# Attention beside a gated MLP on one core: early down products, P.V held for zero products, and two output tiles summed by DMA

## The chip, the cores and the metric

The kernel runs on one core of a Trainium2 chip. The metric is the device time of one execution in microseconds. The engines have their own instruction queues: TensorE (PE, with its weight loads shown as PEld), VectorE (DVE), ScalarE (ACT), GpSimd (POOL) and SyncE (SP). Each takes its instructions in the order in which the program was built; between engines, and between an engine and a DMA, semaphores hold an instruction until what it needs is there.

## The reference

```python
# x: (1, 2048, 640) bf16; wqkv 640x1920, wo 640x640; w_gate, w_up 640x1728, w_down 1728x640
xn = layernorm(x)
# A: 32 heads of 20 columns, full softmax over 2048 keys
q, k, v = split(xn @ wqkv)
s = (softmax(q @ k.T * 20**-0.5) @ v) @ wo
# B: gated MLP
h = sigmoid(xn @ w_gate) * (xn @ w_up)
g = silu(h @ w_down)
out = x + s * g
```

## The kernel before

The 2048 tokens are four chunks of 512 queries, the 32 heads eight groups of four. A **pass** is one chunk with one group: 64 **banks** of scores, each 128 keys of one head by the chunk's 512 queries, in one bank of PSUM. TensorE computes the scores (`score`, L1280), in rounds of three banks and of two in turn (the tiles `sc`). ScalarE takes the exp of a round in one instruction (L1306). Some banks go one at a time to a shared bank (`spare`), and VectorE evaluates the exp by a polynomial in four instructions (L1326, L1347, L1351, L1357). The product of the probabilities with V (P.V, `pv`, L1483) adds all 16 key tiles of a pass into one bank, `oacc`; column 0 of V is one, so that its row holds the denominator. Then VectorE copies `oacc` (L804), the denominators go through DRAM to be inverted and spread (L808 to L824), and L836 scales.

Everything else is a **job**, a generator that gives TensorE's work in small steps: k, q and v projections; `gateup_job` (the gate and the up product of 128 of the 1728 columns of the MLP for one chunk: L667; tanh on ScalarE L679; VectorE's product into `hT`, L688); `down_job` (a 512-column slice of h @ w_down, one bank with 14 products for each piece, L717; tanh L726, VectorE L729, a store to DRAM L731); `out_job` (output projection of an earlier chunk, L751, multiplied by the stored gate value L757, and added by DMA into an output that already holds x, L759). Jobs share two banks of PSUM (`misc0` and `misc1`, `take_bank`) with the `spare` banks of VectorE's exps. The last of a chunk pair's 14 gate and up tiles, 64 columns wide, is computed for two chunks at once, so odd chunks have it from the even chunk before.

The order of all this is not written out: a planner at build time (the loop from L1514) keeps modelled clocks of TensorE, ScalarE and VectorE, and prices in ns (L365 on, `mm_time` L695). At each turn it issues the next round of scores if ScalarE will run dry, else a step of a job (`fill`), a bank for VectorE, a batch of eight P.V products (`pv_batch`), or a product of zeros (`zero_add`, L1454). Zero products keep TensorE's clock up: they are added when less than 2500 ns of products streamed in the last 3400 ns (`streamed`). They go into `oacc` while it has an open sum of P.V (L1459); if all P.V of the pass is issued and `oacc` is not yet copied, they go into an unused shared bank (L1465). `spare_wanted` (L468) keeps one of the two shared banks back from jobs when a round is near, for VectorE.

The last chunk is special, so that little stays behind the last exp. Its gate values stay in SBUF (`gq_last`), in space of `kT_all`. `part_job` multiplies the output projection of the first five groups by the gate for each of four tiles of 128 tokens into `ahead` (two halves of 320 columns, L783 and L788) and adds x by a GpSimd DMA (L791). The last pass is split into parts of 256, 128 and 128 queries (`PARTS`); `last_job` normalises a part on chip (copy of `oacc` L895 or, for the last, L897 on ScalarE; transposes of it L922, inverse L928, spreading L933, product L950, scaling L957), then multiplies the last three groups' projection (`out_mm`, L912) by the gate in halves (`gated`, L997) or, for the last tile, in one (L979). `summed` (L1001) adds `ahead` on VectorE, casts to bf16, and SyncE stores the tile (L1002).

Of the kernel before, what the change touches and what calls it, by code (L numbers as in the profile page):

```python
# [12 lines left out]
ALU = mybir.AluOpType  # L13
# [45 lines left out]
def kernel(  # L59
# [304 lines left out]

    MM5, MM3, MM1 = 216.0, 136.0, 70.0  # L365
    INTO = {"score": 100.0, "pv": 100.0, "fill": 100.0}
    WINDOW, ENOUGH, ZEROS, RESTED = 3400.0, 2500.0, 16, 400.0
    PE_OUT, SEM = 260.0, 70.0
    EXP_COL, EXP_FIX, EXP_LAG = 1 / 1.2, 52.0, 260.0
    DMA_WAIT, LANDED = 3400.0, 4000.0  # L370
# [97 lines left out]
    def spare_wanted():  # L468

        free = sum(c.t is not None and c.t <= pe[0] for c in banks)  # L470
        return (free == 1 and not pressed() and next_round[0] - pe[0] < (KEEP_SPARE if at_bank[0] < SPARE_END else KEEP_LATE)
                and dve.backlog + dve.t - next_round[0] < D_BACKLOG)

    EARLY = 2
# [218 lines left out]
            h_cells.setdefault(c + k, []).append(tnh_free[-1])  # L693

    def mm_time(n):  # L695
        return max(n / 2.4 + 3.0, 100.0)

    def down_pieces(k):
        return [(t4, max(t4 * D, k * QC), min((t4 + 1) * D, (k + 1) * QC)) for t4 in range(QC // P)
# [2 lines left out]
    def down_job(c, k):  # L702
        last = c == NQC - 1
        yield "known", lambda: (bulk[0] == NFT and pe[0] > bulk_t[0] + LANDED and len(h_cells.get(c, [])) == NFT
                                and (not last or front() >= PER_PASS * (NG * c + k // 2 + 1)))
        yield "wait", h_cells[c]
        hT = hTs[c]
        if last:
            gq = gq_last[:, k * QC:(k + 1) * QC]
        else:  # L710
            gq = glu[0].tile([P, QC], FP32, tag="gqr", bufs=4, name="gq")
        held, psd = yield "bank",
        for t4, f0, f1 in down_pieces(k):
            for kf in range(NFT):
                rows = slice(0, P) if kf < NFT - 1 else slice(EDGE * (c % 2), EDGE * (c % 2 + 1))
                h_in = hT[:, kf, :] if kf < NFT - 1 else hEs[c]
                nc.tensor.matmul(psd[:, f0 - k * QC:f1 - k * QC], lhsT=h_in[rows, t4 * P:(t4 + 1) * P],  # L717
                                 rhs=glu[1][rows, kf, f0 - t4 * D:f1 - t4 * D], start=(kf == 0), stop=(kf == NFT - 1),
                                 skip_group_check=True)
                yield "mm", mm_time(f1 - f0), (f1 - f0) / 2.4  # L720
        d_cells.setdefault(c, []).append(Cell(pe[0]))
        made = {}

        def tanh():
            made["t"] = wk.tile([P, QC], BF16, tag="tnh", bufs=2, name="td")
            nc.scalar.activation(out=made["t"], in_=psd, func=ACT.Tanh, scale=0.25)  # L726

        def finish():
            nc.vector.scalar_tensor_tensor(out=gq, in0=made["t"], scalar=1.0, in1=psd, op0=ALU.add, op1=ALU.mult)  # L729
            if not last:  # L730
                nc.gpsimd.dma_start(out=gq_dram[c, :, k * QC:(k + 1) * QC], in_=gq)  # L731

        turned = act.add(480.0, [Cell(pe[0] + PE_OUT + 100.0), *tnh_free[-2:-1]], tanh, 0, EXP_LAG)
        tnh_free.append(dve.add(606.0, [turned], finish, 1))
        give_bank(held, tnh_free[-1])
        gq_cells[c, k] = tnh_free[-1]
# [168 lines left out]
    def last_job(u):  # L905
        q0, width = PARTS[u]
        part, n, final = taken_parts[u], width // P, u == len(PARTS) - 1
        tiles = range(q0 // P, (q0 + width) // P)
        qc, made = NQC - 1, {}

        def out_mm(ps, t4, h, g):
            nc.tensor.matmul(ps, lhsT=oTs[qc, g][:, t4 * P:(t4 + 1) * P], rhs=wo_pad[:, g, h * HALF:(h + 1) * HALF],  # L912
                             start=(g == PRE), stop=(g == NG - 1), skip_group_check=True)

        yield "wait", [part["cell"]]
        if final:
            side = psum.tile([P, 3, 512], FP32, tag="sc0", bufs=1, name="side")
            pd, prl = side[:, 0, :], side[:, 1, :]
        else:
            held, pd = yield "bank",  # L920
        for k in range(n):
            nc.tensor.matmul(pd[:, k * P:(k + 1) * P], lhsT=part["oev"][:, k * P:(k + 1) * P], rhs=identf,  # L922
                             start=True, stop=True, skip_group_check=True)
            yield "mm", 330.0, 200.0

        def invert():
            made["rq"] = wk.tile([P, n, GH], FP32, tag="den", bufs=2, name="rq")
            nc.vector.reciprocal(out=made["rq"].rearrange("p t j -> p (t j)"), in_=pd[:, 0:n * P:P // GH])  # L928

        def spread():  # L930
            made["rb"] = glu[0].tile([P, QC], FP32, tag="gqr", bufs=4, name="rb")[:, 0:n * P].rearrange(
                "p (t j i) -> p t j i", t=n, j=GH)
            nc.vector.tensor_copy(out=made["rb"], in_=made["rq"].unsqueeze(3).to_broadcast([P, n, GH, 32]))  # L933

        cell = dve.add(160.0, [Cell(pe[0] + PE_OUT)], invert, -1)
        if not final:
            give_bank(held, cell)
        cell = dve.add(70.0 + n * P, [cell], spread, -1)
        if final:
            spread_last.append(cell)  # L940
            outs = psum.tile([P, 2, 512], FP32, tag="sc1", bufs=1, name="outs")
            for h in range(2):
                for g in range(PRE, NG - 1):
                    out_mm(outs[:, h, 0:HALF], tiles[0], h, g)
                    yield "mm", MM3
        yield "wait", [cell]
        if not final:
            held, prl = yield "bank",
        for k in range(n):
            nc.tensor.matmul(prl[:, k * P:(k + 1) * P], lhsT=made["rb"][:, k, :, :].rearrange("p j i -> p (j i)"),  # L950
                             rhs=identf, start=True, stop=True, skip_group_check=True)
            yield "mm", 330.0, 200.0

        def scale():
            if steps[-1] not in oTs:
                oTs[steps[-1]] = wk.tile([P, QC], BF16, tag="oT", bufs=NG + 3, name="oT")
            nc.vector.tensor_tensor(out=oTs[steps[-1]][:, q0:q0 + width], in0=part["oev"], in1=prl[:, 0:width],  # L957
                                    op=ALU.mult)

        cell = dve.add(70.0 + width, [Cell(pe[0] + PE_OUT)], scale, -1)  # L960
        if not final:
            give_bank(held, cell)
        yield "known", lambda: all((NQC - 1) * 4 + t4 in out_cells for t4 in tiles)
        yield "wait", [cell, ot_cells[steps[-2]]]
        for k, t4 in enumerate(tiles):
            got = []
            if final:
                if k:
                    outs = psum.tile([P, 3, 512], FP32, tag="sc0", bufs=1, name="outs")
                    for h in range(2):  # L970
                        out_mm(outs[:, h, 0:HALF], t4, h, NG - 2)
                        yield "mm", MM3
                for h in range(2):
                    out_mm(outs[:, h, 0:HALF], t4, h, NG - 1)
                    yield "mm", MM3

                def gate(t4=t4, outs=outs):
                    gq = gq_last[:, t4 * D:(t4 + 1) * D].rearrange("p (h d) -> p h d", h=2)
                    nc.vector.scalar_tensor_tensor(out=gq, in0=outs[:, 0:2, 0:HALF], scalar=0.25, in1=gq,  # L979
                                                   op0=ALU.mult, op1=ALU.mult)  # L980

                got.append(dve.add(740.0, [Cell(pe[0] + PE_OUT)], gate, -1))
            else:
                for h in range(2):
                    held, ps = yield "bank",
                    for g in range(PRE, NG):
                        out_mm(ps[:, 0:HALF], t4, h, g)
                        yield "mm", MM3
                    got.append(dve.add(400.0, [Cell(pe[0] + PE_OUT)], lambda t4=t4, h=h, ps=ps: gated(t4, h, ps), 1))
                    give_bank(held, got[-1])  # L990
                got.append(ending)
            dve.add(740.0, [out_cells[(NQC - 1) * 4 + t4], *got],
                    lambda t4=t4: summed(t4), -1 if final else 2)

    def gated(t4, h, ps):
        gq = gq_last[:, t4 * D:(t4 + 1) * D][:, h * HALF:(h + 1) * HALF]
        nc.vector.scalar_tensor_tensor(out=gq, in0=ps[:, 0:HALF], scalar=0.25, in1=gq, op0=ALU.mult, op1=ALU.mult)  # L997

    def summed(t4):
        ot = glu[0].tile([P, QC], FP32, tag="gqr", bufs=4, name="ot").bitcast(BF16)[:, 0:D]  # L1000
# [513 lines left out]
    while pv_pass[0] < len(steps) - 1 + len(PARTS):  # L1514
# [37 lines left out]
        if b0 < NB and not stuck and alone(room):  # L1552
            idle = False
            credit = min(credit + per_bank(b0), 3000.0)
            continue
        batch = pv_batch()
        cost = PV_TIME + (INTO["pv"] if mode[0] != "pv" else 0.0)
        if batch and (cost <= room or held >= HELD):
            pv(batch)
# [62 lines left out]
```

## Time and profile before

| what | value |
|---|---|
| median of 3 runs | 879.56 us (878.5 to 880.36) |
| profiled execution | 878.75 us, its span 877.1 us |
| busy: TensorE, VectorE, ScalarE, GpSimd | 799.4, 837.9, 861.9, 170.0 us |
| exps on ScalarE (L1306) | 711: 355 of three banks, 356 of two |
| exps on VectorE (L1326) | 271 instructions |
| zero products, built | 163 into `oacc` (L1459), 6 into a shared bank (L1465) |
| mean granted TensorE clock | 0.999 |

The span is the time from the first to the last instruction of the profiled execution. Times in the profile's views are microseconds from the span's start. A line of a timeline gives start, length, engine, source line, operation, the tiles written and read, and in brackets the idle time before it with what ended it. Instructions of one engine overlap a little, so a step from start to start is shorter than a length.

### The profile page before, as it was taken

The numbers are of one execution on the slowest core, as the hardware profiler recorded it, in microseconds if no ns is written. First come the engines' busy times: TensorE is split into PE (matmuls) and PEld (weight loads), VectorE is DVE, ScalarE is ACT, GpSimd is POOL, SyncE is SP. The second block draws the span as 40 slices with busy tenths as digits, with TensorE's granted clock in tenths as the row PEclk, the third lists the DMA queues.
The fourth block names the chain that finished last, engine by engine and source line by source line (L and its number), as shares of the span: only waits on it lengthen the run. The fifth ranks groups of instructions, "written<-read, shape, count | busy, mean of one in ns | idle before, by whom it ended". The sixth has DMA issues, their size and how long they took to land.

```text
span 877.1 us, 16778 instructions
## 1 busy us (share of the span) xinstructions
PE 799.4 (91%) x6358; PEld 286.2 (33%) x6440; DVE 837.9 (96%) x1164; ACT 861.9 (98%) x832; POOL 170.0 (19%) x314
## 2 busy tenths in 40 slices
PE   8999899999998999999999999989989989999997
PEld 3434333332222333222223332232223332233344
DVE  7799999999999999999999999999999999999996
ACT  7999999999999999999999999999999999999996
POOL 8401111101111113211101133111112231111110
PEclk9999999999999999999999999999999999999999
DMA  8212231125542124223321235313211443320111
GB/s 320 62 49 66 72 108 36 33 59 142 155 130 68 28 68 108 38 59 74 73 60 39 68 83 86 72 29 84 57 35 50 101 71 80 71 52 21 26 34 47
DMA packets 107303, 63.86 MB, mean 73 GB/s; under 512 B 78674, under 2 KB 101030, under 8 KB 107130
## 3 DMA queue, kind: packets, MB, share of 16 engines
q1 hardware_dynamic: 95270, 46.96, 20.1%
q0 software_dynamic: 11952, 15.83, 8.5%
q8 instruction: 50, 0.82, 0.4%
q14 instruction: 31, 0.25, 0.1%
HBM read 49.94 MB, written 16.11 MB: 75 GB/s over the span
## 4 chain that ended last, share of the span: by engine, by line
ACT 64%; issue 17%; PE 11%; DVE 6%; DMA 1%; POOL 0%; SPq 0%; ACTq 0%; DVEq 0%; POOLq 0%
ACT p L1306 60%; PE sc L1280 3%; ACT tnh L679 3%; PE work L667 2%; PE work L717 2%; PE oacc L1483 2%; DVE du L1351 1%; DVE dy L1326 1%; ACT td L726 1%; DVE p L1357 1%; DVE du L1347 1%; DMA x_sb<-in_A_x_dram 1%; DVE stats L261 1%; POOL x_sb L284 0%; PE oacc L1459 0%
## 5 line engine op out<-in xcount | busy, mean ns | idle before, releaser
L1306 ACT ACTIVATE p<-sc 128x1536 bf16<-128x1536 f32 x711 | 823.1, 1382 | 1.3 <-PE sc L1280 1.2
L1280 PE MATMUL sc<-qT,kT_all 21*128 21x512 bf16 (+2 forms) x1892 | 278.1, 369 | 55.1 <-ACT p L1306 48.0
L1326 DVE TENSOR_SCALAR dy<-spare 128x512 f32<-128x512 f32 x271 | 184.9, 683 | 14.2 <-PE spare L1280 12.0
L1280 PEld LDWEIGHTS <-kT_all 21*128 21x128 bf16 x2176 | 90.4, 91 | 293.8 <-issue 282.5
L1351 DVE SCALAR_TENSOR_TENSOR du<-du,dy 128x1024 f32<-128x1024 f32 (+1 forms) x166 | 169.3, 1021 | 1.3
L1347 DVE SCALAR_TENSOR_TENSOR du<-dy 128x1024 f32<-128x1024 uint16 (+1 forms) x159 | 168.5, 1060 | 1.2
L1357 DVE SCALAR_TENSOR_TENSOR p<-du,dy 128x1024 uint16<-128x1024 f32 (+1 forms) x152 | 167.2, 1100 | 1.4
L1483 PE MATMUL oacc<-p,v_all 128*21 128x512 bf16 (+2 forms) x2176 | 157.2, 370 | 0.6 <-issue 0.3
L1280 PE MATMUL spare<-qT,kT_all 21*128 21x512 bf16 (+2 forms) x284 | 103.7, 373 | 0.5 <-issue 0.3
L808 POOL DMA_DIRECT2D den_dram<-oev x30 | 18.0, 600 | 354.1 <-DVE oev L804 342.7
L717 PE MATMUL work<-wd,hT 128*128 128x512 bf16 (+3 forms) x410 | 75.2, 301 | 1.9 <-DVE dy L1326 1.2
L667 PE MATMUL work<-xnT,wg 128*128 128x512 bf16 (+1 forms) x262 | 74.0, 383 | 1.9 <-issue 0.6
L667 PE MATMUL work<-xnT,wu 128*128 128x512 bf16 (+1 forms) x266 | 69.8, 381 | 2.1 <-DVE dy L1326 0.6
L824 POOL DMA_DIRECT2D rl<-rec_dram x120 | 60.9, 544 | 52.2 <-DMA rec_dram<-den 47.4
L1483 PEld LDWEIGHTS <-v_all 128*21 128x21 bf16 x2176 | 31.8, 90 | 59.3 <-issue 57.3
L1459 PE MATMUL oacc<-xnT,zero 128*128 128x512 bf16 x124 | 42.7, 385 | 3.0 <-issue 2.4
L717 PEld LDWEIGHTS <-hT 128*128 128x128 bf16 x416 | 30.7, 97 | 39.0 <-issue 29.7
L818 POOL DMA_DIRECT2D rec_dram<-den x30 | 16.4, 547 | 132.9 <-DVE den L817 125.1
L679 ACT ACTIVATE tnh<-work 128x512 bf16<-128x512 f32 x54 | 39.3, 728 | 0.0
L138 PE MATMUL work<-xnT,wqd 128*120 128x512 bf16 (+1 forms) x115 | 35.0, 393 | 0.6 <-DVE hT L688 0.3
L688 DVE SCALAR_TENSOR_TENSOR hT<-tnh,work 128x512 bf16<-128x512 bf16 x52 | 35.3, 679 | 0.1
L667 PEld LDWEIGHTS <-wu 128*128 128x128 bf16 (+1 forms) x280 | 23.4, 98 | 36.7 <-issue 18.8
(132 smaller groups left out, 573.7 us busy)
## 6 DMA issues: line engine op xcount, KB each, us to landing
wg<-in_B_w_gate_dram SPq DMA_DIRECT2D x52, 160.0 KB
wu<-in_B_w_up_dram SPq DMA_DIRECT2D x52, 160.0 KB
rl<-rec_dram POOLq DMA_DIRECT2D x120, 64.0 KB, 2.5
qT<-q_dram SPq DMA_DIRECT2D x31, 128.0 KB
gq_dram<-gq POOLq DMA_DIRECT2D x15, 256.0 KB, 2.3
gqr<-gq_dram SPq DMA_DIRECT2D x15, 256.0 KB
kT_all<-k_dram SPq DMA_DIRECT2D x28, 128.0 KB
wd<-in_B_w_down_dram SPq DMA_DIRECT2D x13, 160.0 KB
```

Of the source, the lines that this page charges most:

```text
L667: nc.tensor.matmul(ps[EDGE * k:EDGE * (k + 1), :] if both else ps, lhsT=w[:, kd, 0:EDGE if both else P], rhs=xnT[:, kd, (c + k) * QC:(c + ...
L679: nc.scalar.activation(out=made["t"][0:fsz, :], in_=psg[0:fsz, :], func=ACT.Tanh, scale=0.5)
L717: nc.tensor.matmul(psd[:, f0 - k * QC:f1 - k * QC], lhsT=h_in[rows, t4 * P:(t4 + 1) * P], rhs=glu[1][rows, kf, f0 - t4 * D:f1 - t4 * D], s ...
L824: nc.gpsimd.dma_start(out=t["rl"][32 * j:32 * j + 32, :], in_=rec_dram[n, j:j + 1, :].to_broadcast([32, QC]))
L1280: nc.tensor.matmul(ps[:, c0:c0 + n], lhsT=kT_all[rows, g, kt * P:(kt + 1) * P], rhs=qTs[qc, g][rows, q0:q0 + n], start=True, stop=True, ti ...
L1306: nc.scalar.activation(out=buf.tile(), in_=ps, func=ACT.Exp, bias=EXP_BIAS, scale=exp_scale)
L1326: nc.vector.tensor_scalar(out=pair.y[:, i * 512:(i + 1) * 512], in0=ps, scalar1=LEAST, scalar2=None, op0=ALU.max)
L1347: nc.vector.scalar_tensor_tensor(out=t["u"][:, a:e], in0=t["f"][:, a:e], scalar=CUBE_2, in1=t["f"][:, a:e], op0=ALU.add, op1=ALU.mult)
L1351: nc.vector.scalar_tensor_tensor(out=t["u"][:, a:e], in0=t["u"][:, a:e], scalar=CUBE_1, in1=t["f"][:, a:e], op0=ALU.add, op1=ALU.mult)
L1357: nc.vector.scalar_tensor_tensor(out=t["p"][:, a:e], in0=t["u"][:, a:e], scalar=CUBE_SCALE, in1=t["y"][:, a:e], op0=ALU.mult, op1=ALU.add)
L1459: nc.tensor.matmul(oacc, lhsT=zero, rhs=xnT[:, 0, 0:QC], start=not begun, stop=not begun, skip_group_check=True)
L1483: nc.tensor.matmul(oacc[32 * j:32 * j + 1 + Dh, q0:q0 + width], lhsT=v_all[:, kt, GH * g + j, 0:1 + Dh], rhs=buf.ap[:, i, c0:c0 + width], ...
```

## The change

Five edits, in the planner and in the last chunk's end:

- `down_job` no longer waits for all 14 gate and up tiles of its chunk before it takes a bank: it waits for all but the last, takes the bank, and in front of each product waits for that product's tile. In odd chunks the tile shared by two chunks, made first, is multiplied first.
- `mm_time`, the price of a product of n columns for the planner, loses its floor of 100 ns, and its fixed part becomes 2.7 ns.
- `spare_wanted` keeps a shared bank back only if more than 1500 ns (`STARVED`) streamed in the last window.
- In the main loop, a pass's last P.V batch (all but 2 x 4 of the 64 P.V banks issued) is put off while fewer than 19 banks are held, no job stands in the middle of its products, and neither shared bank is free by the planner's clock. Zeros can then go into `oacc`.
- For output tiles 0 and 1 of the last chunk (part 0), `summed` is left out. When the second half of such a tile has been multiplied, `gated` issues two GpSimd DMAs: one adds the fp32 tile into `ahead`, the other stores `ahead` to the output with a cast.

```diff
-    WINDOW, ENOUGH, ZEROS, RESTED = 3400.0, 2500.0, 16, 400.0
+    WINDOW, ENOUGH, ZEROS, RESTED, STARVED = 3400.0, 2500.0, 16, 400.0, 1500.0
...
-        return (free == 1 and not pressed() and next_round[0] - pe[0] < (KEEP_SPARE if at_bank[0] < SPARE_END else KEEP_LATE)
+        return (free == 1 and not pressed() and streamed() > STARVED and next_round[0] - pe[0] < (KEEP_SPARE if at_bank[0] < SPARE_END else KEEP_LATE)
...
     def mm_time(n):
-        return max(n / 2.4 + 3.0, 100.0)
+        return n / 2.4 + 2.7
...
     def down_job(c, k):
...
-        yield "wait", h_cells[c]
+        made_in = [(NFT - 1 if c % 2 and not i else i - c % 2, x) for i, x in enumerate(h_cells[c])]
+        yield "wait", [x for _, x in made_in[:-1]]
...
         held, psd = yield "bank",
         for t4, f0, f1 in down_pieces(k):
-            for kf in range(NFT):
+            for i, (kf, h_cell) in enumerate(made_in):
+                yield "wait", [h_cell]
...
-                                 rhs=glu[1][rows, kf, f0 - t4 * D:f1 - t4 * D], start=(kf == 0), stop=(kf == NFT - 1),
+                                 rhs=glu[1][rows, kf, f0 - t4 * D:f1 - t4 * D], start=(i == 0), stop=(i == NFT - 1),
...
                 got.append(ending)
+            if u == 0:
+                continue
             dve.add(740.0, [out_cells[(NQC - 1) * 4 + t4], *got],
                     lambda t4=t4: summed(t4), -1 if final else 2)
...
     def gated(t4, h, ps):
         gq = gq_last[:, t4 * D:(t4 + 1) * D][:, h * HALF:(h + 1) * HALF]
         nc.vector.scalar_tensor_tensor(out=gq, in0=ps[:, 0:HALF], scalar=0.25, in1=gq, op0=ALU.mult, op1=ALU.mult)
+        if h == 1 and t4 * P < PARTS[0][1]:
+            part = ahead[:, t4, :]
+            nc.gpsimd.dma_start(out=part, in_=gq_last[:, t4 * D:(t4 + 1) * D], accum_op=ALU.add)
+            nc.gpsimd.dma_start(out=out_view[:, (NQC - 1) * 4 + t4, :], in_=part)
...
         batch = pv_batch()
+        if (batch and b0 < LAST and held < 19 and sum(pv_count[0]) == GH * KT - 2 * GH and not held_job()
+                and all(c.t is None or c.t > pe[0] + 0.0 for c in banks)):
+            batch = None
```

## The prediction

> **What bounds the kernel now.** I read the page first: busy times, then the costliest groups.
>
> ```profile
> span 877.1 us, 16778 instructions
> PE 799.4 (91%) x6358; PEld 286.2 (33%) x6440; DVE 837.9 (96%) x1164; ACT 861.9 (98%) x832; POOL 170.0 (19%) x314
> PEclk9999999999999999999999999999999999999999
> L1306 ACT ACTIVATE p<-sc 128x1536 bf16<-128x1536 f32 x711 | 823.1, 1382 | 1.3 <-PE sc L1280 1.2
> ```
>
> ScalarE is the bound: 711 exps, and in front of them 1.3 us of idle time in all. TensorE has its full clock everywhere, so work that keeps its clock up has nothing to win here. The rows of exps in the trace start 1.33 us apart after one of three banks, 0.90 after one of two, and 0.477 after a tanh of one bank (their durations overlap). 355 x 1.33 + 356 x 0.903 + 74 x 0.477 = 829.0 us, while the stretch from the first exp (27.66) to the last copy on ScalarE (869.31) is 841.7. So all waits of ScalarE, the small ones that the page does not count included, are 12.7 us. Two are large: 0.81 in front of the last copy, for the last P.V, and 0.86 here (the timeline of ScalarE; start, length):
>
> ```profile
> 855.56 2.46 ACT L1306 ACTIVATE p<-sc 128x1536 bf16<-128x1536 f32 x2
> 858.65 2.37 ACT L1306 ACTIVATE p<-sc 128x1536 bf16<-128x1536 f32 x2 [0.64 <-PE sc L1280]
> ```
>
> The timeline of TensorE for the same stretch:
>
> ```profile
> 856.14 1.25 PE L1465 MATMUL unused<-xnT,zero 128*128 128x512 bf16 x3
> 857.46 0.49 PE L922 MATMUL work<-identf,oev 128*128 128x128 f32 x2
> 858.10 0.42 PE L1280 MATMUL sc<-qT,kT_all 21*128 21x128 bf16 x12
> ```
>
> The exp of 858.65 could have begun at 855.56 + 1.33 + 0.90 = 857.79. Three zero products into a spare bank stand in front of its scores; each waits for the one before, so they step by 0.43 instead of the 0.216 of zeros into oacc (859.20: three in 0.82 with the last one's 0.39).
>
> After ScalarE's last copy comes a tail in which the chain runs through VectorE and a store. The timeline of all engines, of which VectorE's lines are these:
>
> ```profile
> 871.30 0.29 DVE L957 TENSOR_TENSOR oT<-oev,side 128x128 bf16<-128x128 f32 x1
> ...
> 871.51 0.82 DVE L1001 TENSOR_TENSOR ot<-kT_all 128x640 bf16<-128x640 f32 x1
> ...
> 872.25 0.82 DVE L979 SCALAR_TENSOR_TENSOR kT_all<-outs,kT_all 128x640 f32<-128x640 f32 x1
> 873.10 0.83 DVE L1001 TENSOR_TENSOR ot<-kT_all 128x640 bf16<-128x640 f32 x1
> ```
>
> SyncE issues the last store at 873.95. It lands at about 875.7 (SyncE's wait for it is 1.3 us), and closing the program takes 1.4 more. So only two places can move the time: waits of ScalarE, and this tail.
>
> **The change, part by part.** I compared the built instructions of both kernels in order; that view holds no time.
>
> *ScalarE's work.* 355 exps of three banks in both; 356 of two become 355, and one of a single bank is new: the last. One bank more goes to VectorE. That is 0.903 - 0.477 = 0.43 us less, at the last exp. But between the last P.V and the transposes of the last part, TensorE now has six products for output tile 1 instead of three. Before, the transposes began at 869.64 right after ScalarE's copy (869.59) with the three products just done; a product steps by 0.134 (three of L912 in 0.58, the last 0.31), so three more push the transposes by 0.40. Together -0.03: nothing.
>
> *Down products early, narrow products priced lower, the bank kept back only when TensorE streamed enough.* These move fillers from the first chunk's down products on; the counts of real products stay. A down product of 128 columns steps by 0.057 (302.79: seven in 0.56, the last 0.22), so the new price of 56 ns is the true one where 100 stood; 104 + 48 such products, 6.7 us of TensorE's time, had been planned for and not used. What hides all this is ScalarE's queue of work: TensorE must only deliver scores in time, and it does so but for the waits above. Setting aside the two large ones, 11.0 us of small waits over 711 exps remain, about 35 of them 0.1 to 0.35 us. The new order re-deals them. Adding up the steps of TensorE's products between neighbouring rounds of scores gives nearly the same loads in both (254 of 711 gaps hold more than ScalarE's step less 0.3 us before, 261 after). I take 0, and keep -1 to +1.3.
>
> *The held P.V batch and zeros.* Zeros into oacc go from 163 to 185, the six into a spare bank go away. The 16 more are 16 x 0.216 = 3.5 us, in TensorE's idle time (55 us in front of scores). If that cover were gone, up to 3.5 us of it would show as waits. Where the three serial zeros stood, the new order has five products of the fourth output tile: the wait goes, **-0.86**. Next in line there are rounds as full as their neighbours, without a wait of their own.
>
> *VectorE* loses two sums (0.82 each) and gains a bank's evaluation, some of it in halves: off the path, since the tail's VectorE is idle between its steps. In the tail the gate (872.25) can start when its products are out, 871.65 + 0.45 + 0.09 = 872.19: the store of tile 3 gains 0.06.
>
> *Two tiles by DMA.* Here is the cost. GpSimd's queue gets four DMAs behind each other: add tile 0, store tile 0, add tile 1, store tile 1. Each store reads what its add wrote, so the queue stands until the add has landed, and tile 1's add stands behind tile 0's store. And in the new order the second half of tile 1 is multiplied by VectorE only behind the last part's scaling: just where L1001 began at 871.51. Rows for the DMAs are, first, the view of line L791, the fp32 add of an input tile into the same buffer:
>
> ```profile
> L791 POOL DMA_DIRECT2D kT_all<-in_A_x_dram x4: 858/898/930, 821.2 to 855.3; - x4
> ...
> DMA to landing us min/median/max: 3.8/3.8/3.9
> ```
>
> Then that of line L731, a plain fp32 store of 256 KB:
>
> ```profile
> L731 POOL DMA_DIRECT2D gq_dram<-gq x15: 539/563/575, 305.0 to 691.0; - x15
> ...
> DMA to landing us min/median/max: 2.3/2.3/2.5
> ```
>
> GpSimd issues 0.30 after VectorE's end (L791, L808) and 0.29 after a landing it waits for (L813). No add from SBUF to SBUF is in the trace: between 2.6 and 4.2 (the adds of L759), and I take 3.8, the same destination and size. The store casts to bf16: between 2.3 (the plain store) and 3.3 (the median of L759), and I take 2.5, near the plain one.
>
> Tile 0: its second half is ready at about 867.3 (its products stand between the last two rounds of scores); add issued 867.6, landed 871.4, store issued 871.7 to 872.3. Tile 1: half ready 871.51 + 0.49 = 872.00, add issued 872.30 (the queue is free just then), landed 876.10, store issued 876.39, **landed 878.89** against 875.7. Closing takes some 1.15 then, since four of SyncE's closing waits, 0.06 each, now stand in front of that landing: 880.04, or +2.94.
>
> *The sum*: +2.94 - 0.86 - 0.03 + 0 = **+2.1 us** on the profiled execution, whose time is 878.75 (1.65 around its span): 880.8. The median of the runs shown, 879.56, is 0.8 above it; I forecast the median, **881.6**. Bounds of the DMAs: 3.3 + 2.3 gives +1.4, 4.2 + 3.3 gives +3.3.
>
> The Trainium skill ("DMA: Bandwidth & Descriptors", Anatomy of one DMA) has one price for a GpSimd DMA, 2.0 us + bytes / 436 GB/s, adding or not; an estimate from it is 2.75 for each of the two, and +1.3 in place of +2.1. The rows here speak against one price: 3.8 with an add, 2.3 without.
>
> **Rivals.**
> 1. *The adds cost what a plain store costs.* Then tile 1 lands at 872.30 + 2.3 + 0.29 + 2.3 = 877.19, and the sum is +0.4: **880.0**, not slower. For it: source and destination are both in SBUF, and L791's 3.8 contains a read of device memory. Against it: the quickest add of L759 already takes 2.6. It decides once both together take under 5.9 us, since +1.76 (0.2%, about what a measurement of this kernel can tell from no change) is then not reached. Chance 0.20. (The Trainium skill's single price, above, would end in this case too.)
> 2. *ScalarE's small waits shrink.* With true prices TensorE is nowhere late by plan; if half of the 11.0 go, the sum is 2.1 - 5.5 = -3.4: **876.2**, faster. It decides from 3.9 us of waits saved. Against it: the plan was too careful before, which idles TensorE but does not make scores late, and the loads between rounds hardly differ. Chance 0.07.
> 3. *The small waits grow*, by some 3 us: a down product that began early holds one of only two shared banks until the last tile arrives, and 16 more zeros stand in front of scores. 2.1 + 3 = +5.1: **884.7**. Against it: VectorE takes as many banks as before, one more. Chance 0.13.
>
> **How the numbers follow.** The forecast's case has 0.60: its own range is +1.4 to +3.3 and a turn of -1 to +1.3 for the waits, so 0.46 of it is beyond +1.76 and 0.14 within. Slower 0.46 + 0.13 = 0.59; same 0.14 + 0.20 = 0.34; faster 0.07. The range goes from rival 1 less the spread of the runs shown (0.6) to the high bound of the DMAs plus 1.3: 879.4 to 884.2.
>
> **What would show it.** ScalarE's last exp starts about 0.8 earlier than 867.6 and is of one bank; no wait near 858; no product into a spare bank. The chain that ended last ends in GpSimd's two stores, the queue waiting for an add about 3.5 us twice; SyncE's last store lands some 3 us before the end. I am wrong if the add takes under 3 us, if tile 1's half is multiplied before the last part's scaling, or if ScalarE's waits differ from 11 us by more than 2.

## The result

| | before | changed |
|---|---|---|
| median | 879.56 us | **882.19 us** (881.74 to 884.88, seven runs) |
| ratio | | 1.0042 (95%: 1.0026 to 1.0058): slower, by 0.4% |
| profiled execution, its span | 878.75, 877.1 us | 882.03, 880.3 us |
| last copy on ScalarE, from the first exp | 841.66 us | 840.71 us |
| ScalarE's waits but for the large ones (two before: 0.81 and 0.86; one after: 0.85, in front of the last copy) | 10.98 us | 11.27 us |
| last landing of a GpSimd store | none in the tail | 878.88 us |

Three of the changed kernel's seven runs took 2.8 us more than the other four, at a mean granted TensorE clock of 0.992 in place of 0.996 to 0.997; experiments 7 to 12 bear on that.

The page of the changed kernel, in the lines that were shown of before:

```profile
span 880.3 us, 16817 instructions
PE 800.2 (91%) x6370; PEld 286.9 (33%) x6456; DVE 836.2 (95%) x1168; ACT 861.6 (98%) x832; POOL 173.1 (20%) x318
PEclk9999999999999999999999999999999999999998
L1314 ACT ACTIVATE p<-sc 128x1536 bf16<-128x1536 f32 x711 | 821.8, 1376 | 0.7 <-PE sc L1288 0.6
```

ScalarE has 711 exps as before and waits 0.6 us less for scores in the profile's own count (0.7, 1.3 before). The 8 at the end of the clock's row is new: TensorE idles while transfers end the program. The timeline of ScalarE has no break any more where it waited at 858.65:

```profile
849.18 18.73 ACT L1314 ACTIVATE p<-sc 128x1536 bf16<-128x1536 f32 x17
868.46 0.28 ACT L899 ACTIVATE oev<-oacc 128x128 f32<-128x128 f32 x1 [0.55 <-PE oacc L1491]
```

So ScalarE is done 0.85 us earlier on the span's clock (868.46 for 869.31), and the program still ends 3.2 us later. VectorE's part of the tail, and GpSimd's timeline:

```profile
870.89 0.48 DVE L1001 SCALAR_TENSOR_TENSOR kT_all<-work,kT_all 128x320 f32<-128x320 f32 x1
871.51 0.82 DVE L981 SCALAR_TENSOR_TENSOR kT_all<-outs,kT_all 128x640 f32<-128x640 f32 x1
872.37 0.83 DVE L1009 TENSOR_TENSOR ot<-kT_all 128x640 bf16<-128x640 f32 x1
```

```profile
867.65 0.85 POOL L1004 DMA_DIRECT2D kT_all<-kT_all  x1 [5.06 <-ACT p L1314]
871.54 0.56 POOL L1005 DMA_DIRECT2D out_dram<-kT_all  x1 [3.04 <-DMA kT_all<-kT_all]
872.09 0.90 POOL L1004 DMA_DIRECT2D kT_all<-kT_all  x1
876.41 0.56 POOL L1005 DMA_DIRECT2D out_dram<-kT_all  x1 [3.42 <-DMA kT_all<-kT_all]
```

Each L1005 stands behind the landing of its L1004: the brackets of 3.04 and 3.42 us are the queue waiting. The third line has no bracket: it did not wait for data (tile 1's half was ready at 870.89 + 0.48 = 871.37) but for the queue, which the store held until 872.09. The view of line L1004 gives the landing:

```profile
DMA to landing us min/median/max: 3.6/3.7/3.8
```

L1005 lands 2.5 after its issue, at 878.88; SyncE's last store has landed at 876.3. The chain of work that ended last names the same place:

```profile
871.58 0.52 POOL out_dram L1005
872.09 3.77 DMA kT_all<-kT_all
875.86 0.03 issue
875.88 0.02 POOLq L1005
875.90 0.48 issue
876.38 0.59 POOLq L1628
```

One transfer of 3.77 us stands on the path by itself, and 0.55 between its landing and the store that needs it. Behind that store's landing the program still takes 1.44. The view of line L1628, the closing of the program, says what it waits for there:

```profile
L1628 POOLq DRAIN  x3: 46/93/3160, 876.4 to 880.1; - x3
```

The longest of the three is the first, GpSimd's instruction DRAIN: it begins at 876.38 and ends at 879.54, 0.66 behind the landing. SyncE has its own waits and drains behind it at 879.19; the next step of the closing, on all engines, comes at 879.72.

### The profile page after: what moved, and what is told of

It is laid out like the page before. It is cut to its first block, busy times and chain, and to the rows that moved or that the text cites. A ratio compares the mean times of both kernels' runs of the same rounds, so it can differ in the third digit from the quotient of the medians.

```text
span 880.3 us, 16817 instructions
## 1 busy us (share of the span) xinstructions
PE 800.2 (91%) x6370; PEld 286.9 (33%) x6456; DVE 836.2 (95%) x1168; ACT 861.6 (98%) x832; POOL 173.1 (20%) x318
## 4 chain that ended last, share of the span: by engine, by line
ACT 58%; issue 17%; PE 12%; DVE 10%; DMA 1%; POOL 1%; SPq 0%; POOLq 0%; ACTq 0%; DVEq 0%
ACT p L1314 54%; PE sc L1288 4%; ACT tnh L679 3%; PE work L667 2%; DVE dy L1334 2%; PE oacc L1491 2%; DVE du L1359 2%; DVE p L1365 2%; DVE du L1355 2%; ACT td L728 1%; PE work L719 1%; DMA x_sb<-in_A_x_dram 1%; DVE stats L261 1%; PE oacc L1467 1%; DVE hT L688 1%
## 5 line engine op out<-in xcount | busy, mean ns | idle before, releaser
L1334 DVE TENSOR_SCALAR dy<-spare 128x512 f32<-128x512 f32 x272 | 185.8, 683 | 14.2 <-PE spare L1288 12.7
L719 PE MATMUL work<-wd,hT 128*128 128x128 bf16 (+3 forms) x408 | 75.2, 300 | 1.4 <-issue 0.8
L1467 PE MATMUL oacc<-xnT,zero 128*128 128x512 bf16 x145 | 48.5, 385 | 2.3 <-issue 1.6
```

The costliest lines, as they stand in the source:

```text
L1334: nc.vector.tensor_scalar(out=pair.y[:, i * 512:(i + 1) * 512], in0=ps, scalar1=LEAST, scalar2=None, op0=ALU.max)
L1467: nc.tensor.matmul(oacc, lhsT=zero, rhs=xnT[:, 0, 0:QC], start=not begun, stop=not begun, skip_group_check=True)
```

## Experiments

The theory: four serial GpSimd transfers make the end late, the vanished wait gives 0.85 us back, and the planner's edits do little else. The rival: the planner's edits cost time. The kernel before ran 100 times beside the experiments: 52 runs from 878.1 to 879.4 us, with a median of 878.87, and 48 from 879.8 to 886.1. The ratios below hold all of them; where a kernel's undisturbed time is compared, it is with 878.87.

**1. VectorE's sums, planner edits kept** (e1).

```diff
-            if u == 0:
-                continue
...
-        if h == 1 and t4 * P < PARTS[0][1]:
-            part = ahead[:, t4, :]
-            nc.gpsimd.dma_start(out=part, in_=gq_last[:, t4 * D:(t4 + 1) * D], accum_op=ALU.add)
-            nc.gpsimd.dma_start(out=out_view[:, (NQC - 1) * 4 + t4, :], in_=part)
```

> The changed kernel with one part undone: VectorE sums all four output tiles and SyncE stores them, as before; the planner's edits stay. Theory (the serial GpSimd transfers are the whole loss; the planner's edits give back 0.85 us through the zero products that no longer end in a spare bank): profiled span 877.1 - 0.85 = 876.2 us, median 878.7, ratio to before 0.999. Rival (the replanned fillers or the new waits cost the time): the loss stays, 881 us or more. On the 2.8 us by which three of the changed kernel's seven runs are longer at a granted clock of 0.992: if the replanned fillers let the clock drop, some runs here show it too; if it belongs to the tail, none does.

Measured: median 879.18, ratio 0.9994 (0.9983 to 1.0006), span 877.2. The loss is gone, but the gain did not arrive: eleven of the twelve runs are undisturbed, and their median, 879.17, is 0.3 above 878.87. The last copy is 0.95 us earlier from the first exp, as in the changed kernel; VectorE then uses it up:

```profile
870.67 0.48 DVE L999 SCALAR_TENSOR_TENSOR kT_all<-work,kT_all 128x320 f32<-128x320 f32 x1
871.07 0.81 DVE L1003 TENSOR_TENSOR ot<-kT_all 128x640 bf16<-128x640 f32 x1
871.80 0.82 DVE L981 SCALAR_TENSOR_TENSOR kT_all<-outs,kT_all 128x640 f32<-128x640 f32 x1
872.53 1.55 DVE L1003 TENSOR_TENSOR ot<-kT_all 128x640 bf16<-128x640 f32 x2
```

Two sums (x2) are left behind the gate L981 where before had one, because the planner's new order multiplies the last halves of tiles 0 and 1 later (866.36 and 870.67). VectorE ends at 874.08, against 873.93 before. Without the transfers, VectorE is the tail's bound.

**2. The transfers alone** (e2): before, with the edits of `gated` and of the sums, and nothing else.

```diff
+            if u == 0:
+                continue
...
+        if h == 1 and t4 * P < PARTS[0][1]:
+            part = ahead[:, t4, :]
+            nc.gpsimd.dma_start(out=part, in_=gq_last[:, t4 * D:(t4 + 1) * D], accum_op=ALU.add)
+            nc.gpsimd.dma_start(out=out_view[:, (NQC - 1) * 4 + t4, :], in_=part)
```

> The kernel before with the GpSimd sums of two output tiles as the one edit. Theory: the tail is four transfers in a row. Tile 0's half is ready about 866.1, its add issued 0.3 to 0.6 later and landed 3.6 later at 870.2; its store issued 870.5 to 871.1; the second add behind it at 871.1, landed 874.9; its store issued 875.2 to 875.4 and landed 2.5 later at 877.9; closing 1.4: span 879.3 us, 2.2 more than before, median 881.8, ratio 1.0025. Rival (transfers hidden behind SyncE's last store, which landed 875.7 before): ratio 1.000. No run at a granted clock of 0.992, if that comes from the planner's edits.

Measured: median 882.76, ratio 1.0035 (1.0022 to 1.0049), span 879.9: +2.8 us of span by this part alone, 0.6 more than expected. GpSimd's timeline:

```profile
870.66 0.56 POOL L1003 DMA_DIRECT2D out_dram<-kT_all  x1 [3.04 <-DMA kT_all<-kT_all]
871.20 0.90 POOL L1002 DMA_DIRECT2D kT_all<-kT_all  x1
875.97 0.56 POOL L1003 DMA_DIRECT2D out_dram<-kT_all  x1 [3.87 <-DMA kT_all<-kT_all]
```

Tile 1's half was ready early here, and its add stood behind the first store (871.20, with no idle time in front); it took 4.2 us. Together with 1, this puts the loss in the transfers.

**3. Only tile 0 by transfers** (e3).

```diff
-            if u == 0:
+            if u == 0 and t4 == 0:
...
-        if h == 1 and t4 * P < PARTS[0][1]:
+        if h == 1 and t4 == 0:
```

> The changed kernel with only output tile 0 summed by GpSimd's transfers; tile 1 goes back to VectorE. Theory: the price of the change sits in the second pair of transfers. Tile 0's store lands at about 874.0, ahead of SyncE's last store, which moves by at most one 0.5 us sum to 875.0 to 875.7 and sets the end again: span 876.3 to 877.0 us, median 878.7 to 879.5, ratio 0.999 to 1.000. Rival (GpSimd's use by itself prolongs the end, by its drain or by contention with SyncE's stores): span 878 us or more.

Measured: **878.22**, ratio 0.9981 (0.9972 to 0.9991), span 876.6: it beats both kernels. None of its twelve runs is a long one; against before's undisturbed runs the gain is 0.65 us, the rest of the ratio is that before has long runs. GpSimd's last line, and VectorE's:

```profile
871.57 0.56 POOL L1005 DMA_DIRECT2D out_dram<-kT_all  x1 [3.04 <-DMA kT_all<-kT_all]
873.04 0.83 DVE L1009 TENSOR_TENSOR ot<-kT_all 128x640 bf16<-128x640 f32 x1
```

Tile 0's store lands at 874.1 and GpSimd's drain ends at 874.64, both ahead of SyncE's last store (875.7): they are hidden. One of VectorE's sums is gone from the tail, which ends 873.87 with tile 3's. It has the lowest median of this study; that of experiment 5 is 0.4 higher, and the intervals of their ratios overlap.

**4. Both adds, then both stores** (e4).

```diff
-            nc.gpsimd.dma_start(out=out_view[:, (NQC - 1) * 4 + t4, :], in_=part)
+            for t in range(2) if t4 else ():
+                nc.gpsimd.dma_start(out=out_view[:, (NQC - 1) * 4 + t, :], in_=ahead[:, t, :])
```

> The changed kernel with GpSimd's four transfers in another order: both adds, then both stores. Theory (tile 1's add waited 0.65 us for the queue that tile 0's store held): the second add is issued at about 871.67 instead of 872.09, lands at 875.45; two stores follow, the first issued at 876.0, the second 0.6 to 0.9 later, which lands at 879.1 to 879.4 because both stores now stand behind the second add: span 880.2 to 880.8 us, no gain on the changed kernel's 880.3. If a store's issue costs the queue nothing, the last one lands at 878.4 and the span is 879.8. Rival (order is of no matter, the end is set elsewhere): the same span with the add issued no earlier.

Measured: 881.51, ratio 1.0027 (1.0015 to 1.0039), span 879.8. GpSimd's timeline:

```profile
871.77 0.86 POOL L1004 DMA_DIRECT2D kT_all<-kT_all  x1 [3.16 <-DVE kT_all L1001]
872.30 0.89 POOL L1006 DMA_DIRECT2D out_dram<-kT_all  x1
875.92 0.55 POOL L1006 DMA_DIRECT2D out_dram<-kT_all  x1 [2.73 <-DMA kT_all<-kT_all]
```

The add now waits for its data (the bracket names VectorE's L1001, 0.30 after its end at 871.47), and the end comes 0.5 earlier: 0.33 by the earlier issue, and 0.17 because this add took 3.60 us in place of 3.77. My main figure was wrong: tile 0's store does not stand behind the second landing, since its own add had landed at 871.35; it is issued at 872.30 beside the second add.

**5. A GpSimd addition in place of the transfers** (e5).

```diff
-            part = ahead[:, t4, :]
-            nc.gpsimd.dma_start(out=part, in_=gq_last[:, t4 * D:(t4 + 1) * D], accum_op=ALU.add)
-            nc.gpsimd.dma_start(out=out_view[:, (NQC - 1) * 4 + t4, :], in_=part)
+            ot = glu[0].tile([P, QC], FP32, tag="gqr", bufs=4, name="ot").bitcast(BF16)[:, 0:D]
+            nc.gpsimd.tensor_tensor(out=ot, in0=gq_last[:, t4 * D:(t4 + 1) * D], in1=ahead[:, t4, :], op=ALU.add)
+            nc.sync.dma_start(out=out_view[:, (NQC - 1) * 4 + t4, :], in_=ot)
```

> The changed kernel with tiles 0 and 1 summed by a GpSimd addition of 128x640 in place of its transfers, and stored by SyncE. Theory: two DMA latencies in a row are the price, not GpSimd. GpSimd's one priced neighbour is an 874 ns scaling of 128x640 bf16; at 0.9 to 1.8 us for this one, tile 1's sum ends by 871.4 + 0.3 + 1.8 = 873.5 and its store goes out beside tile 3's, which VectorE ends at 873.2: span 876.0 to 876.6 us, median 877.7 to 878.3, ratio 0.998. Rival (GpSimd's access to the buffers holds VectorE up, or the drain at its end delays the closing): VectorE's last sum ends after 873.9, span 877 or more.

Measured: 878.59, ratio 0.9985 (0.9969 to 1.0000), span 876.8. GpSimd's work is not the price, two DMA latencies in a row are. The rival had a share, though. VectorE's last sum and GpSimd's second:

```profile
872.33 1.36 DVE L1009 TENSOR_TENSOR ot<-kT_all 128x640 bf16<-128x640 f32 x1
```

```profile
871.47 1.53 POOL L1004 TENSOR_TENSOR ot<-kT_all 128x640 bf16<-128x640 f32 x1 [2.75 <-DVE kT_all L1001]
```

The same sum takes 0.83 in the changed kernel. Here it ends 0.69 after GpSimd's at 873.00, about as if it had begun there. The Trainium skill ("SBUF — State Buffer", SBUF: two separate sides) says that VectorE with two inputs in SBUF and GpSimd exclude each other for a whole instruction; this pair of rows agrees, and the gate L981, with one input in PSUM, kept its 0.82 beside GpSimd.

**6. One transfer, with the earlier sum stored ahead** (e6), and **7. the same, stored late** (e8). The output then gets the earlier sum in bf16 first.

```diff
                     nc.gpsimd.dma_start(out=part, in_=x_view[:, tt, :], accum_op=ALU.add)
+                    if t4 * P < PARTS[0][1]:
+                        nc.gpsimd.dma_start(out=out_view[:, tt, :], in_=part)
...
-            nc.gpsimd.dma_start(out=part, in_=gq_last[:, t4 * D:(t4 + 1) * D], accum_op=ALU.add)
-            nc.gpsimd.dma_start(out=out_view[:, (NQC - 1) * 4 + t4, :], in_=part)
+            nc.gpsimd.dma_start(out=out_view[:, (NQC - 1) * 4 + t4, :], in_=gq_last[:, t4 * D:(t4 + 1) * D],
+                                accum_op=ALU.add)
```

> The changed kernel with one transfer behind each of the two tiles' halves: the earlier sum is stored in the output ahead of the end, and the last gated half is added to the output in DRAM. Theory (a serial pair of latencies is the price): tile 1's add goes out at 871.7, with tile 0's issued at 867.6 and out of the queue's way; the same kind of add took 2.6 to 4.2 us, median 3.3, earlier in the kernel, so it lands at 874.3 to 875.9; closing 1.4 or tile 3's store at 876.0 ends it: span 876.3 to 877.5 us, ratio 0.998 to 1.000. Rival (anything on GpSimd's queue so late costs the 3 us, through the drain or the closing): span 879 or more.

Measured: 883.14, ratio 1.0041 (1.0025 to 1.0057), span 882.2. The tail did what was expected: from tile 1's half to the end 5.5 us, against 8.95. But the stretch from 829 us on lost 5.4. GpSimd's timeline of that stretch, the waits in it, and the table by stages (width; busy PE, PEld, DVE, ACT, POOL; granted clock; DMA):

```profile
827.82 0.56 POOL L795 DMA_DIRECT2D out_dram<-kT_all  x1 [3.02 <-DMA kT_all<-in_A_x_dram]
828.37 0.57 POOL L817 DMA_DIRECT2D den<-den_dram  x1
```

```profile
DVE den L821 <- DMA den<-den_dram: 3.3, 1, 3.3
...
PE work L719 <- DVE dy L1335: 2.7, 1, 2.7
```

```profile
829.00:832.00 3.00, 1.14 (x14) 0.72 (x15) 1.18 (x2) 3.00 (x4) 0.55 (x1) 1.00 0.35 54
832.00:835.00 3.00, 2.20 (x12) 0.33 (x11) 3.00 (x4) 0.10 (x1) 1.01 (x2) 0.54 0.06 11
835.00:839.00 4.00, 4.00 (x12) 0.82 (x10) 3.13 (x5) 2.48 (x2) 0.99 (x2) 0.50 0.15 33
```

The new store waits in GpSimd's queue for the add in front of it. The load of the denominators, issued at 824.49 in the changed kernel, goes out at 828.37 behind it; VectorE stands 3.3 us at L821 for it, TensorE 2.7 for a shared bank that VectorE has not emptied. Then the granted clock falls to half for 6.8 us. A wait put into an in-order queue cost more than the two latencies that it was to save.

For e8, against the changed kernel:

```diff
-        if h == 1 and t4 * P < PARTS[0][1]:
...
+        if t4 * P < PARTS[0][1]:
+            gq = gq_last[:, t4 * D:(t4 + 1) * D]
+            nc.gpsimd.dma_start(out=out_view[:, (NQC - 1) * 4 + t4, :], in_=gq if h else ahead[:, t4, :],
+                                accum_op=ALU.add if h else ALU.bypass)
```

> As e6, one transfer behind each of the two halves, but the earlier sum of a tile is stored when its first gated half goes out (864.4 for tile 0), not in the stretch where GpSimd's queue carries the normaliser's transfers. Theory: the 5.4 us that e6 lost around 835 us were waits for that store in the in-order queue and go; what stays is e6's tail, whose time from tile 1's half to the end was 5.5 us against 8.95 in the changed kernel: 871.4 + 5.5 = 876.9 us of span, 877.7 if the second store still in the queue holds the last add up by one 0.8 us issue; median 878.6 to 879.5. Rival (the late store is waited for in the queue as the sums were, so two latencies stand in a row again): span 879 to 880.5.

Measured: 880.03, ratio 1.0005 (0.9992 to 1.0017). The profiled span, 880.9, holds another fall of the clock (480.4 to 487.2, waits of ScalarE 2.97 in all); without it some 877.9, by an estimate that takes off these waits. The tail is 6.7 us, not 5.5: tile 1's early store is issued behind the first add at 871.0 and lands at 875.0, and the last add is issued at 875.58, though its half is ready at 874.22. Part of the rival: two latencies overlap the half's arrival instead of standing wholly behind it.

**8. Without the three zero products** (e7): before, with no products into a spare bank in the last pass; the planner's clocks unchanged. It leaves out nothing that the output needs.

```diff
-            ps = psum.tile([P, QC], FP32, tag=f"misc{free[0]}", bufs=1, name="unused")
-            nc.tensor.matmul(ps, lhsT=zero, rhs=xnT[:, 0, 0:QC], start=True, stop=True)
+            if at_bank[0] < LAST:
+                ps = psum.tile([P, QC], FP32, tag=f"misc{free[0]}", bufs=1, name="unused")
+                nc.tensor.matmul(ps, lhsT=zero, rhs=xnT[:, 0, 0:QC], start=True, stop=True)
```

> The kernel before, with one thing left out: the three zero products into a spare bank at 856.14 (1.25 us), which nothing reads; the planner's own times and everything else stay. Theory: these three hold up the next scores, for which ScalarE waited 0.86 us at 858.65; without them that wait goes, ScalarE's last copy comes 0.85 us earlier, and since tile 0's sum stays early here (866.5 before), the whole tail moves with it: span 876.2 us, ratio 0.999. Rival (the wait moves on to the next thing that is late, VectorE's polynomial for the last pass): last copy moved by less than 0.3, span 877. If the plan of fillers decides how often the clock falls, runs over 880 us stay as frequent as in the kernel before (about 15 of 33).

Measured: 880.40, ratio 1.0013 (0.9987 to 1.0039); its shortest runs are 878.49 and 878.50, which shows no gain by itself, since before's shortest are 878.13 and 878.28. The trace does: the wait of 0.86 shrank to one of 0.48 at 859.58, only half of the gain, and neither theory nor rival had that. Most of its runs were longer, and the profiled one shows why it was. The table by stages, first before, then e7:

```profile
293.00:296.00 3.00, 2.00 (x13) 0.60 (x10) 3.00 (x6) 3.00 (x3) 0.58 (x1) 1.00 0.02 3
296.00:299.00 3.00, 3.00 (x25) 0.83 (x23) 2.87 (x4) 3.00 (x4) 0.56 (x1) 1.00 0.02 3
```

```profile
293.00:296.00 3.00, 2.05 (x12) 0.61 (x8) 3.00 (x6) 3.00 (x3) 0.58 (x1) 0.81 0.02 3
296.00:299.00 3.00, 3.00 (x18) 0.64 (x17) 2.18 (x2) 1.82 (x3) 0.57 (x1) 0.62 0.03 3
```

The two programs are the same there. In one execution the clock stayed at 1.00; in the other it was half from 294.9 to 298.3, and ScalarE's busy time fell from 3.00 to 1.82 of 3 us, with waits of 1.67. Counted at the 0.216 us by which products of 512 columns step (those that run side by side once), columns stream in only 1.4 us of the 3.4 us from 291.5 on; in the changed kernel and e3 in 2.2. (Before's trace shows 1.25, but it has one record fewer: one product of zeros at 294.50, where e7's has two.)

Why one program falls in one execution and not in another is argued, not shown. In every trace the changes of the clock stand a multiple of 3.413 us apart, on a grid that lies elsewhere in each execution. The step in front of e7's fall is 291.46 to 294.87 and holds the thin stretch (1.4 us). Before's trace changes its clock at 876.05; counted back from there, its step is 292.37 to 295.78, which takes in the down products from 294.95 on (1.6 us, with the missing record added).

**9 to 12. The planner's edits one by one**, with VectorE's sums: the lines of `down_job` alone (p_only_dn), of the held batch alone (p_only_hd), of `mm_time` alone (p_only_mm), and all but those of `down_job` (p_no_dn). `STARVED` has no run of its own: taken out of the changed kernel or put into before by itself, it leaves the built program as it is. Against before, cut to their core, in this order:

```diff
-        yield "wait", h_cells[c]
+        yield "wait", [x for _, x in made_in[:-1]]
...
-            for kf in range(NFT):
+            for i, (kf, h_cell) in enumerate(made_in):
+                yield "wait", [h_cell]
```

```diff
+        if (batch and b0 < LAST and held < 19 and sum(pv_count[0]) == GH * KT - 2 * GH and not held_job()
+                and all(c.t is None or c.t > pe[0] + 0.0 for c in banks)):
+            batch = None
```

```diff
-        return max(n / 2.4 + 3.0, 100.0)
+        return n / 2.4 + 2.7
```

p_no_dn is e1 with the first of these taken back.

> The kernel before with the early down products as the one edit. Theory: by itself it leaves two zero products into a spare bank near the end in place of three, so 0.0 to 0.4 us of the 0.85 us gain on ScalarE; small waits unchanged at 11 us; span 876.7 to 877.2, ratio 1.000. Rival (a down product that stands in a shared bank for the last tile costs ScalarE): small waits grow by 1 us or more, ratio 1.001 or above. On the clock: if this edit is what makes the runs at a lower clock rare, at most 2 of its runs are over 880 us.

> The kernel before with the hold of a pass's last P.V batch as the one edit. It has four zero products into a spare bank (six before), three of them still near the end, and a last exponential of one bank for two. Theory: no gain by itself at the end, 0 to 0.4 us; small waits of ScalarE about 11 us, span 876.7 to 877.3, ratio 1.000. Rival (the hold delays products that ScalarE's scores need): small waits above 12 us, ratio 1.001 or more. The fall of the clock at 293 to 299 us goes if the hold fills TensorE's gap there.

> The kernel before with the planner's shorter time for narrow products as the one edit. It has four zero products into a spare bank in a row near the end, and a last exponential of one bank for two. Theory: four in a row (1.7 us) hold the next scores up longer than three did, wait of ScalarE there 0.9 to 1.3 us, small waits elsewhere about 11: span 877.0 to 877.6, ratio 1.000 to 1.001. Rival (the planner now believes narrow products shorter than they are and sends scores late): small waits above 12 us.

> All the planner's edits but the early down products, with VectorE's sums; no zero product goes into a spare bank. If the edits add up, the down edit's 1.2 us of small waits is what the other two made good in e1, and without it ScalarE's waits fall from e1's 12.1 to 10.9 us, the last copy comes 1.2 us earlier still, span 876.0. If they do not add up (each edit deals the fillers out anew), ScalarE's waits land anywhere between 11 and 14 us, and no edit has a price of its own. I take the second as likelier, as the counts of zero products (2, 4 and 9 alone, none together) do not add up either.

| edits | median | ratio (95%) | shortest run less 878.87 | ScalarE's waits | falls of the clock in the trace |
|---|---|---|---|---|---|
| `down_job` | 882.87 | 1.0029 (1.0008 to 1.0050) | +1.1 | 15.2 | 295.6 to 299.0 |
| held batch | 880.37 | 1.0008 (0.9994 to 1.0022) | +1.1 | 13.1 | none |
| `mm_time` | 882.45 | 1.0031 (1.0016 to 1.0046) | +2.5 | 17.2 | 294.9 to 298.3 |
| all but `down_job` | 883.76 | 1.0052 (1.0033 to 1.0071) | +3.3 | 17.5 | 653.3, 830.8 (3.4 each) |
| all (e1) | 879.18 | 0.9994 (0.9983 to 1.0006) | +0.1 | 12.1 | none |

Before has 12.7 us of these waits. The fourth column sets a shortest run against a median, so it is a lower bound of the cost; before's own shortest run is at -0.7. By itself each edit makes the kernel slower (the ratio of the held batch alone does not tell, but none of its runs is below 879.95); together they cost about 0.3 (e1). The edits do not add up: each deals the fillers out anew. With the held batch alone ScalarE also has two banks of exps more (356 rounds of three, 355 of two, one of one): 0.90 us by the steps of its exps. Expectations that gave an edit about zero (1.000) were wrong for `down_job` and `mm_time`, whose rivals came in, and for the span of the held batch (878.7, expected up to 877.3). For p_no_dn the second branch held in kind, but waits of 11 to 14 us are met only without the two falls (4.0 of the 17.5), and 2.2 us of its loss lie behind the last copy, where three sums stand in a row at the end. From experiments 8 to 12 a second effect is seen: the place at 295 us, where the clock fell in three of the traces (e7, p_only_dn, p_only_mm; up to it their products are those of before), is filled by the held batch (2.2 us streamed in 3.4, no fall) and by all edits together. That before's long runs come from a fall at this place too is likely (their granted clock is mostly 0.995 to 0.998, that of the others mostly 0.998 to 1.000), but no trace here is of such a run.

## Why the prediction was right, and where it was not

- *Two tiles by DMA, the cost that decides.* Right. An add from SBUF to SBUF took 3.6 and 3.77 us, for 3.8; the casting store 2.48, for 2.5; tile 1's half is multiplied behind the last scaling. Rival 1 needed both under 5.9; they took 6.25. The transfers are the cause of the loss: alone they cost 2.8 us of span (experiment 2), without them the loss is gone (experiments 1 and 5), and it is gone as well when only tile 1's pair is left out (experiment 3).
- *"The queue is free just then."* This step failed. It was written for a half ready at 872.00, ahead of the 0.86 taken off later in the sum; taken off first, the half comes while the store of tile 0 holds the queue. Cost +0.43; experiment 4, by another order, issued that add 0.33 earlier.
- *Issue 0.29 after a landing.* For this store 0.55 (+0.26). It is not the kind of store: tile 0's was issued 0.28 after its landing. Why the two differ stays open. *Closing 1.15*: 1.44 (+0.29). The sum counted SyncE's waits; the closing waits for GpSimd's drain, which ends 0.66 behind the landing. With 0.15 for the half and 0.10 for a later first exp, these are the 1.2 by which the profiled span grew more (880.3) than the sum said (877.1 + 2.1).
- *The wait of 0.86.* It goes, and the changed kernel has no product into a spare bank. That the three products alone made it is refuted: without them half stays (experiment 8). The order behind them counts as much.
- *ScalarE's last exp and the transposes, -0.03.* The exp is of one bank (-0.43), as said. The transposes began 0.43 after the last copy's end in place of 0.05, so 0.38 later, close to the 0.40 of the sum; but the pair then took 0.38 us in place of 0.49, and the inverse behind it came only 0.22 later. Small waits took 0.3. In all VectorE's inverse came 0.73 earlier from the first exp, for 0.89 in the sum.
- *Small waits at 0.* Measured 11.27 for 10.98. The sum held, by luck: "the new order re-deals them" is what happens, and it comes out even only for all edits together. Rival 2 (3.9 us less) did not come. The 3 us of rival 3 did for `mm_time` alone (17.2, of which 1.4 are a fall of the clock, against 12.7); whether by its mechanism is not shown.
- *"TensorE has its full clock everywhere, so work that keeps its clock up has nothing to win here."* Wrong as a statement on the kernel: it was read from one execution. In the traces of e7, p_only_dn and p_only_mm a fall at 295 us costs 1.4 to 1.7. The changed kernel and e1, e3, e4, e5, e6 and e8 have TensorE's program in common; of their 79 runs 12 took over 2 us more than their kernel's shortest (from none of 12 in e3 to three of 7 in the changed kernel), of before's 100 runs 43. The filled gap is probably a gain of the planner's edits that the sum left out, and one reason why the medians lie 2.6 apart and the undisturbed times 882.0 and 878.87 lie 3.1 apart.
- *The number.* That 881.6 lies only 0.6 below the measured 882.19 is in part luck. The sum missed 1.2 us of the tail; the 879.56 that it was added to holds long runs and stands 0.7 above before's undisturbed 878.87. Two of its signs were off for the same reasons: the last exp began at 867.13, 0.47 earlier and not 0.8, and SyncE's last store landed 4.0 us before the end, not 3.

Not settled: where the clock fell in the changed kernel's three long runs. e8's fall at 480 us costs about the same 3 us, and TensorE's program, in its order, is the same in both; that it is the same place is argued, not shown.

## What to carry to other kernels

Behind the last compute, count latencies in a row, not bytes: an add by DMA that another DMA must wait for puts two of them there, while one sum of VectorE costs 0.8 us. Of two equal pieces, send away the one whose transfers have landed before the rest ends (tile 0), and keep the other. When a queue is taken in order, compute the arrival at it after all earlier shifts of the sum, and ask what stands behind each new wait; and before saying that a clock or a gap does not matter, look at more than one execution.

## What the hardware showed unexpectedly

- TensorE's clock fell to half for one step of 3.41 us or two, after a step of 3.41 us in which columns streamed for 0.8 (e6), 1.3 (p_only_mm), 1.4 (e7, p_only_dn), 1.7 and 1.8 (p_no_dn) and 1.8 us (e8). Before's step with 1.6 us passed without a fall, so the streamed time gives no sharp bound here. The Trainium skill ("TensorE: Matmul & The Clock Gate", Part 1: The HAM clock gate) gives a free-running window of 3413 ns, which the steps agree with, and half clock after an idle window; none of the steps named above was idle.
- One step at half clock costs ScalarE 1.4 to 2.3 us of waits; two in a row cost 3.0 (e8), or 5.4 with the stall that led to them (e6).
- A GpSimd addition of two fp32 tiles of 128x640 took 1.53 to 1.55 us, VectorE's 0.82 to 0.83.
- An add by DMA with source and destination in SBUF is no quicker than one from device memory into SBUF: 3.6 to 3.8 us, once 4.2 (e2), against 3.7 to 3.9 in the same three kernels (changed, e2, e4).
- GpSimd's drain at the end of the program ended 0.66 us behind the landing of the last DMA that GpSimd had issued, where that was the last of all (the changed kernel, e2, e4, e8), and the closing waited for it.
